# Two hand-overs of a fused attention and MoE kernel: weight pools freed in four parts, and a first output pair of eight plain products

## The chip, the cores and the metric

The kernel runs on one core of one Trainium2 chip. The metric is the device time of one execution in microseconds (us), less being better; all inputs start in the chip's memory and the output ends there. The core's engines are TensorE (PE in the profile), VectorE (DVE), ScalarE (ACT), GpSimd (POOL) and SyncE (SP), which mostly issues DMA transfers.

## The reference

Three stages, float32 in and out; the weights come as float64.

```python
B, H, S, D = 4, 8, 576, 64
scores = q @ k.T / sqrt(D) + min(bias(cumsum(max(s, 0))), 0)      # causal
x = softmax(scores) @ v            # to (2304 tokens, 512)
h = max(x @ w1, x @ w2, x @ w3)    # MoE1, three gates, d_ff 768
x = h @ w_out                      # (2304, 512)
a, b = x @ w_a, x @ w_b            # MoE2, d_ff 1536
out = (a * b) @ w_out2             # (2304, 512)
```

## The kernel before

**Products.** Each float32 operand is held as a rounded high part and the rest as a low part (`hi` and `lo`), and a product of two operands is three matmuls (hi·hi, hi·lo, lo·hi), added up in PSUM. The function `hilo` (L841) makes the two: `rnd` rounds on ACT (L81) or POOL (L88), then DVE subtracts (it is recorded at L839, as all of DVE's sums are).

**Stages.** Attention and MoE1 are interleaved until about 512 us. MoE1 keeps 22 of its 24 weight slabs (18 gate slabs, 6 of `w_out`; hi and lo of a slab are 4 KB in a partition) in one pool, `w1p` (L102, L247). For each block of 256 or 320 tokens it runs 18 gates of 12 matmuls (L555) and four `o` units of 18 (L582). Each `o` unit ends with an ACT copy into `xo` (L587) and a store by SP into the DRAM tensor `x2T` (L588). `xo` has two buffers, shared with the gates' `hf`.

MoE2's gates and the output are Strassen-Winograd products: of two 2x2 block matrices seven products are formed instead of eight, from sums of blocks that `a_side` and `b_side` make on DVE. MoE2 has 12 column blocks `c` and three token blocks `sb` of 768; a unit (c, sb) is a `Unit` (from L958) with the products 1, 2, 5, 6, 7, 4 and 3 of six matmuls with 384 columns. The products of one unit gather in three PSUM banks X, Y and Z with two buffers each: 1, 6, 7 and 4 go to X, 2 to Y, 5 and 3 to Z; between them ACT copies X out (`s1`, `u2`, `u3`; L981 to L987), and DVE adds. `emit` puts product 4 and 3 of the unit before between those of the next. A unit's two results are stored into `hT`, in DRAM (L1016, L1020).

x of token block 0 is split (`x2_part`) while MoE1 still runs. Those of blocks 1 and 2 (the halves of the tile `xt12`) are loaded at L909 in the first two units of MoE2, each with seven roundings, on ACT and POOL in turn, seven low parts and four sums on DVE. Their pools lie over `w1p`, and `xt12` also. w2(c), the weights of column block c, come as pairs of 32-bit words: a load into `wraw` (L825), an ACT pass (L828), two DVE passes (L831, L833), and `b_side` with POOL's roundings.

The output runs over nine pairs of 128-token blocks. `load_h` reads four pieces of `hT` into `hraw0` or `hraw1` (L1120), `prep_h` splits it with `a_side` into `slot` tiles, and seven products of 18 matmuls with 256 columns follow. Its weights (`wo32`, four blocks b11 to b22) are split by `b_side` into `woh1` to `wol7`.

**Order.** The kernel is written in program order with pools of tiles; a scheduler reorders the instructions by a simulated timeline, helped by `high_priority` blocks, and each engine then executes its list in order. A pool made with `reuse_waits="tile"` lets a new tile wait only for what lay under it; what was in one pool over several old ones waits per tile.

Of the kernel before, what the change touches and what calls it, by code (L numbers as in the profile page):

```python
# [29 lines left out]
def kernel(  # L30
# [29 lines left out]
    P = 128  # L60
# [41 lines left out]
    w1p = tc.alloc_tile_pool(name="w1p", bufs=1, side="left")  # L102
# [144 lines left out]
    w1_tiles(w1p, w1_keys[: NPRE - MF])  # L247
# [292 lines left out]
    def moe1_units(R, b, X):  # L540
# [31 lines left out]
        def outp(c):  # L572
# [15 lines left out]
            nc.sync.dma_start(x2T[c * P : (c + 1) * P, col : col + n], xo[:, :n])  # L588
# [212 lines left out]

    TB = 384
# [11 lines left out]
    def to_f32(src, outs):  # L814
# [23 lines left out]
    def tt(e, o, a, b, op):  # L838
        {"V": nc.vector, "P": nc.gpsimd}[e].tensor_tensor(o, a, b, op=op)  # L839

    def hilo(eng, hi, lo, src):  # L841
        rnd(eng, hi, src)
        tt("V", lo, src, f(hi), ALU.subtract)


# [82 lines left out]
    w1p.release()  # L928
# [361 lines left out]
```

## Time and profile before

| | us |
|---|---|
| median of 3 executions | 946.49 |
| lowest, highest | 943.96, 951.84 |
| the profiled execution | 949.84 |
| its span | 947.6 |
| PE busy | 904.0 (95% of the span) |
| DVE busy | 600.6 (63%) |
| ACT busy | 383.5 (40%) |
| POOL busy | 227.7 (24%) |

The profile is of one execution, and its times are on the clock of its span. A row of a chain of waits or a timeline names the engine, the line of the kernel, the operation and the tiles (out<-in), and says what the engine waited for before it. L839 and L81, L88 are helpers' lines, so the tile's name tells what the instruction is for. The granted clock is the share of TensorE's full speed that the chip granted in a stretch.

### The profile page before, as it was taken

Reading aid. Unit: us, or ns where it says so; the run is one execution under the profiler, and the core shown is the slowest. Engines: PE = TensorE matmul, PEld = TensorE weight load, DVE = VectorE, ACT = ScalarE, POOL = GpSimd, SP = SyncE. Lnnn points to the kernel's source line nnn. Section 1 sums busy time; section 2 is a strip of 40 time slices with the busy share of each in tenths; the row PEclk is TensorE's granted clock in tenths of the full one; section 3 lists DMA queues with packets and bytes.
Section 4 is the critical chain, followed back from the end, with each engine's and each line's share of the span. In section 5 each row is a group of like instructions: output and inputs, shape, how many; then the busy total and the mean of one; then the engine's idle time right before and its main releaser. Section 6 shows DMA issues by size and latency. Waiting matters only on the chain.

```text
span 947.6 us, 16918 instructions
## 1 busy us (share of the span) xinstructions
PE 904.0 (95%) x6182; PEld 841.6 (89%) x6182; DVE 600.6 (63%) x1416; ACT 383.5 (40%) x878; POOL 227.7 (24%) x331
## 2 busy tenths in 40 slices
PE   5899999999999999999999799999999998699998
PEld 4587789989999899999898699999999998699998
DVE  4787445554464644555563977666665779778874
ACT  4555644555455554555322323232322133233321
POOL 5454311222132221222111411111111212121220
PEclk9899999999999999999999999999999999799999
DMA  6655232313213132220314325353522131543431
GB/s 172 209 178 177 86 80 81 95 40 116 76 56 93 58 99 77 61 76 30 122 56 141 134 79 193 118 164 121 170 95 95 67 109 41 185 145 118 150 112 45
DMA packets 55210, 102.34 MB, mean 108 GB/s; under 512 B 5736, under 2 KB 39432, under 8 KB 55128
## 3 DMA queue, kind: packets, MB, share of 16 engines
q1 hardware_dynamic: 55128, 101.26, 34.0%
q8 instruction: 49, 0.80, 0.3%
q14 instruction: 33, 0.27, 0.1%
HBM read 77.29 MB, written 23.94 MB: 107 GB/s over the span
## 4 chain that ended last, share of the span: by engine, by line
PE 72%; DMA 12%; DVE 11%; issue 2%; ACT 1%; SPq 1%; POOL 0%; ACTq 0%; DVEq 0%
PE g L555 22%; PE X L952 15%; PE Z L952 7%; PE o L582 7%; PE fpv L500 5%; PE Y L952 4%; DMA wraw<-in_moe_w_b_dram 3%; DMA wraw<-in_moe_w_out_dram 3%; PE t L514 3%; PE f L435 2%; DVE u L839 2%; PE s L391 2%; DVE xl L839 2%; PE s L392 1%; DVE wl L839 1%
## 5 line engine op out<-in xcount | busy, mean ns | idle before, releaser
L555 PE MATMUL g<-Xh,hg 128*128 128x256 f32 (+1 forms) x576 | 176.3, 309 | 2.5 <-ACT hf L561 1.4
L555 PE MATMUL g<-Xl,hg 128*128 128x256 f32 (+1 forms) x576 | 174.9, 304 | 0.3 <-DVE Xl L92 0.2
L555 PE MATMUL g<-Xh,lg 128*128 128x256 f32 (+1 forms) x576 | 174.0, 303 | 0.0
L555 PEld LDWEIGHTS g<-Xh,hg 128*128 128x128 f32 x576 | 109.6, 191 | 6.6 <-ACT hf L561 1.6
L555 PEld LDWEIGHTS g<-Xl,hg 128*128 128x128 f32 x576 | 110.0, 191 | 3.0 <-DVE Xl L92 1.2
L555 PEld LDWEIGHTS g<-Xh,lg 128*128 128x128 f32 x576 | 109.8, 191 | 2.5 <-issue 2.3
L952 PE MATMUL X<-xh,wh 128*128 128x384 f32 x288 | 98.5, 342 | 8.3 <-ACT u L987 3.5
L952 PE MATMUL X<-xh,wl 128*128 128x384 f32 x288 | 97.3, 338 | 0.4 <-DVE wl L839 0.3
L952 PE MATMUL X<-xl,wh 128*128 128x384 f32 x288 | 97.0, 337 | 0.4 <-DVE xl L839 0.4
L88 POOL TENSOR_SCALAR wh<-wval 128x256 fp32r<-128x256 f32 x84 | 41.1, 499 | 218.2 <-PE Z L952 151.0
L952 PE MATMUL X<-woh,slot 128*128 128x256 f32 x432 | 83.5, 285 | 6.7 <-ACT slot L81 6.3
L564 DVE TENSOR_TENSOR hf<-g,hf 128x256 f32<-128x256 f32 (+1 forms) x96 | 43.7, 455 | 60.3 <-PE g L555 55.7
L952 PEld LDWEIGHTS X<-woh,slot 128*128 128x128 f32 x432 | 69.8, 193 | 7.3 <-ACT slot L81 6.6
L839 DVE TENSOR_TENSOR slot<-hraw,slot 128x768 fp32r<-128x768 f32 x63 | 62.7, 1014 | 18.3 <-POOL slot L88 16.6
L384 POOL TENSOR_SCALAR P<-P,rs 128x128 f32<-128x128 f32 (+2 forms) x80 | 51.0, 642 | 92.1 <-DVE rs L380 63.1
L952 PEld LDWEIGHTS X<-xh,wh 128*128 128x128 f32 x288 | 54.1, 188 | 12.9 <-ACT u L987 4.7
L952 PE MATMUL X<-wol,slot 128*128 128x256 f32 x216 | 61.3, 285 | 0.0
L375 ACT ACTIVATE P<-P,nm 128x128 f32<-128x128 f32 (+2 forms) x80 | 46.5, 581 | 32.2 <-DVE nm L368 26.6
L88 POOL TENSOR_SCALAR slot<-hraw 128x768 fp32r<-128x768 f32 x27 | 27.6, 1022 | 129.0 <-DVE hraw L839 53.1
L582 PE MATMUL o<-hh,lo 128*128 128x256 f32 (+1 forms) x192 | 58.2, 309 | 0.0
L81 ACT ACTIVATE slot<-hraw 128x768 fp32r<-128x768 f32 x36 | 30.4, 847 | 68.1 <-DVE hraw L839 36.0
L582 PE MATMUL o<-hl,ho 128*128 128x256 f32 (+1 forms) x192 | 57.6, 303 | 0.0
(156 smaller groups left out, 2267.2 us busy)
## 6 DMA issues: line engine op xcount, KB each, us to landing
hT<-u SPq DMA_DIRECT2D x72, 192.0 KB
hraw<-hT SPq DMA_DIRECT2D x36, 384.0 KB
wraw<-in_moe_w_dram SPq DMA_DIRECT2D x18, 512.0 KB
wraw<-in_moe_w_out_dram SPq DMA_DIRECT2D x18, 512.0 KB
qvraw<-in_qv_dram SPq DMA_DIRECT2D x12, 640.0 KB
kraw<-in_kT_dram SPq DMA_DIRECT2D x24, 288.0 KB
wraw<-in_moe_w_a_dram SPq DMA_DIRECT2D x12, 512.0 KB
wraw<-in_moe_w_b_dram SPq DMA_DIRECT2D x12, 512.0 KB
```

The source lines that it names most:

```text
L81: nc.scalar.activation(o, i, AF.Copy, scale=scale)
L88: nc.gpsimd.tensor_scalar(o, i, scale, 1.0, op0=ALU.mult, op1=ALU.mult)
L375: nc.scalar.activation(pt[:, c0:c1], pt[:, c0:c1], AF.Exp, bias=first, scale=-1.0, accum_out=sm[:, g : g + 1],)
L384: nc.gpsimd.tensor_scalar(pt[:, c0:c1], pt[:, c0:c1], rs[:, g : g + 1], 1.0, op0=ALU.mult, op1=ALU.mult,)
L391: nc.tensor.matmul(ps, QA1[:, qs], KB1[:, h, ksl], start=True, stop=False)
L500: nc.tensor.matmul(ps[h * D : h * D + D, c0:n], w, x, start=(t == 0), stop=(t == len(mm[h]) - 1),)
L514: nc.tensor.transpose(ps[:, j * P : j * P + P], pt[:, j * P : j * P + P], ident)
L555: nc.tensor.matmul(ps[:, :n], w[:, kk, :], x[:, kk, :], start=(i == 0), stop=(i == len(mm) - 1),)
L564: nc.vector.tensor_tensor(hf, ps[:, :n], hf, op=ALU.max)
L582: nc.tensor.matmul(ps[:, :n], w[:, c, :], x[:, m, :n], start=(i == 0), stop=(i == len(mm) - 1),)
L839: {"V": nc.vector, "P": nc.gpsimd}[e].tensor_tensor(o, a, b, op=op)
L952: nc.tensor.matmul(ps[:, :n], w, x, start=(first and i == 0), stop=(i == len(mm) - 1), skip_group_check=not first,)
```

## The change

The diff is cut to what decides places and order. Its parts:

1. `w1p` becomes four pools of 6, 5, 7 and 4 slabs (24, 20, 28 and 16 KB), and the pools of MoE2 are placed over them so that `xt12` lies over the first, the second raw buffer, w2(1) and five of the seven products of x1 over the second and third; products 7 and 3 of x1 have a pool of their own over the fourth.
2. The stores into `x2T` are issued by ACT instead of SP.
3. A weight's raw load is a step of its own (`load_raw`); that of w2(2) is written ahead of MoE2. Weight tiles are one for each product.
4. x1 is rounded by POOL alone, x2 by ACT alone; x2's loads are written in the third unit, behind w2(2)'s load and x1's last split. Units (0,2) and (1,1) change places.
5. The output's first pair is eight plain products of split blocks, in four chains of 36 matmuls (`out_std`), with no sums of blocks; the Winograd pairs begin with the second. The tiles of the output have other places, `hraw1` among them, which lay over x2 and now lies over MoE2's first raw buffer and weights.

```diff
-    w1p = tc.alloc_tile_pool(name="w1p", bufs=1, side="left")
+    w1p = [tc.alloc_tile_pool(name=f"w1p{i}", bufs=1, side="left") for i in range(4)]
-    w1_tiles(w1p, w1_keys[: NPRE - MF])
+    for p_, n0, n1 in zip(w1p, (0, 6, 11, 18), (6, 11, 18, NPRE - MF)):
+        w1_tiles(p_, w1_keys[n0:n1])
...
             nc.scalar.copy(xo[:, :n], ps[:, :n])
-            nc.sync.dma_start(x2T[c * P : (c + 1) * P, col : col + n], xo[:, :n])
+            nc.scalar.dma_start(x2T[c * P : (c + 1) * P, col : col + n], xo[:, :n])
...
-    def to_f32(src, outs):
+    def load_raw(src):
         pool = rawp[nraw[0] % len(rawp)]
         nraw[0] += 1
         raw = pool.tile([P, WC, 2], I32, tag="raw", bufs=1, name="wraw")
+        rv = raw.rearrange("p c t -> p (c t)")
...
+        return raw, nc.sync.dma_start(rv, src.bitcast(I32))
+
+    def to_f32(raw, outs):
...
-        nc.sync.dma_start(raw.rearrange("p c t -> p (c t)"), src.bitcast(I32))
...
     def hilo(eng, hi, lo, src):
         rnd(eng, hi, src)
-        tt("V", lo, src, f(hi), ALU.subtract)
+        return tt("V", lo, src, f(hi), ALU.subtract)
+    def a_side(q, sp, part=(0, 1)):
...
+        if 0 in part:
+            sp(1, a11)
...
+        if 1 in part:
+            sp(6, a11)
...
+    w2raw = {}
+
+    def load_w2_raw(c):
+        w2raw[c] = [load_raw(src[c]) for src in (wa, wb)]
+        return w2raw[c][1][1].ins
...
-        hi, lo = (
-            pool.tile([P, 7, 2 * P], F32R, tag=f"w{x}", bufs=1, name=f"w{x}{c % 2}")
-            for x in "hl"
-        )
+        hi, lo = {}, {}
+        for i in OPS:
+            for d, x in ((hi, "h"), (lo, "l")):
+                d[i] = pool.tile(
+                    [P, 2 * P], F32R, tag=f"w{x}{i}", bufs=1, name=f"w{x}{i}_{c % 2}"
+                )
         v_ = rA.tile([P, 4, 2 * P], F32, tag="val", bufs=1, name="wval")
-        for src, s in ((wa, 0), (wb, 2)):
-            to_f32(src[c], [(v_[:, s : s + 2].rearrange("p s c -> p (s c)"), slice(0, WC))])
+        for n, src in enumerate((wa, wb)):
+            raw = w2raw[c][n] if c in w2raw else load_raw(src[c])
+            o = v_[:, 2 * n : 2 * n + 2].rearrange("p s c -> p (s c)")
+            to_f32(raw[0], [(o, slice(0, WC))])
...
         if sb not in xs:
-            xs[sb] = [
-                {i: xr[sb].tile([P, KH, TB], F32R, name=f"x{c}{sb}{i}") for i in OPS}
-                for c in "hl"
-            ]
+            xs[sb] = {}, {}
+            for i in (1, 2, 4, 6, 5, 7, 3):
+                pool = xr1b if sb == 1 and i in (7, 3) else xr[sb]
+                for d, c in zip(xs[sb], "hl"):
+                    d[i] = pool.tile([P, KH, TB], F32R, name=f"x{c}{sb}{i}")
...
-    w1p.release()
+    for p_ in reversed(w1p):
+        p_.release()
...
     wop = lpool("wop")
     xt12 = wop.tile([P, 2, 4, KH, TB], F32, tag="wo", name="xt12")
+    rawB = lpool("rawB")
+    rawB.tile([P, WC, 2], I32, tag="raw", bufs=1, name="raw1")
+    wpool[1] = lpool("wB")
     xr[1] = lpool("xr1")
+    xr1b = lpool("xr1b")
     tmpA = lpool("tmpA")
-    tmpA.tile([P, WC, 2], I32, tag="raw", bufs=1, name="raw1")
-    rawp.append(tmpA)
-    wpool[1] = lpool("wB")
     xr[2] = lpool("xr2")
     ps_w = lpool("ps_w", space=PSUM)
...
-    order = [(0, 0), (1, 0), (0, 1), (0, 2), (1, 1), (1, 2)]
+    done1 = []
+
+    def load_x1():
+        done1.append(x2_part(1, 0, KH, xt12[:, 0], "P"))
+
+    def load_x2():
+
+
+        with tc.issue_after(raw2), tc.issue_after(done1[0]):
+            x2_part(2, 0, KH, xt12[:, 1], "A")
+
+    order = [(0, 0), (1, 0), (0, 1), (1, 1), (0, 2), (1, 2)]
     load_w2(1)
+    rawp.append(rawB)
+    raw2 = load_w2_raw(2)
         extra = []
-        if n < 2:
-            extra.append(lambda n=n: x2_part(n + 1, 0, KH, xt12[:, n], "AP"))
+        if n == 0:
+            extra.append(load_x1)
+        if n == 2:
+            extra.append(load_x2)
...
+    slots = {}
+
+    def put(pool, i0, i1):
+        for i in range(i0, i1):
+            slots[i] = pool.tile([P, KO, P], F32R, name=f"slot{i}")
...
     rB1 = rpool("rB1")
-    wo_tiles(rB1, ("l6", "h6", "l5", "h5"))
-    rB1.tile([P, 1024], F32, name="pad1")
+    wo_tiles(rB1, ("h6", "l6"))
+    obs = ob_tiles(rB1, 0, 2)
+    hraw1 = rB1.tile([P, MF2, 2 * P], F32, name="hraw1")
     rB2 = rpool("rB2")
-    hraw = [rB2.tile([P, MF2, 2 * P], F32, name="hraw0")]
-    wo_tiles(rB2, ("h1", "l1", "h2", "l2", "h3"))
+    hraw = [rB2.tile([P, MF2, 2 * P], F32, name="hraw0"), hraw1]
+    wo_tiles(rB2, ("h1", "l1", "h2", "l2"))
+    lB0 = lpool("lB0")
+    wo_tiles(lB0, ("h5", "l5", "h4"))
     lB1 = lpool("lB1")
-    wo_tiles(lB1, ("l3",))
-    slots = [lB1.tile([P, KO, P], F32R, name=f"slot{i}") for i in range(12)]
+    put(lB1, 0, 8)
+    wo_tiles(lB1, ("h3", "l3"))
+
+    wo7_tiles(0)
     lB2 = lpool("lB2")
-    slots += [lB2.tile([P, KO, P], F32R, name=f"slot{i}") for i in range(12, 18)]
-    wo_tiles(lB2, ("h7", "l7", "h4", "l4"))
-    hraw.append(lB2.tile([P, MF2, 2 * P], F32, name="hraw1"))
+    put(lB2, 8, 18)
+    wo_tiles(lB2, ("l4",))
...
+    def prep_std(blocks, engs):
+
+        r = hraw[0]
+        for b, e in zip(blocks, engs):
+            c, k = b // 2 * P, b % 2 * KO
+            hilo(e, slots[2 * b], slots[2 * b + 1], r[:, k : k + KO, c : c + P])
+
+    def out_std():
+
+        gate = prev[0]
+        o = obs[0], obs[1]
+        t0 = porder[0] * 2 * P
+        banks = dict(zip(((0, 0), (0, 1), (1, 1), (1, 0)), "XYZX"))
+        for (r, c), b in banks.items():
+            ps = ps_w.tile([P, 512], F32, tag=b, bufs=2, name=b)
+            mm = []
+            for k2 in range(2):
+                i = {(0, 0): 1, (1, 0): 2, (0, 1): 0, (1, 1): 3}[k2, c]
+                hh, hl = slots[2 * (2 * r + k2)], slots[2 * (2 * r + k2) + 1]
+                wh, wl = wot[f"h{i}"], wot[f"l{i}"]
+                for k in range(KO):
+                    mm += [
+                        (hh[:, k], wh[:, k]), (hh[:, k], wl[:, k]), (hl[:, k], wh[:, k]),
+                    ]
+            chain(ps, True, 256, mm)
+            nc.scalar.copy(o[r][:, 256 * c : 256 * c + 256], ps[:, :256])
+            if (r, c) == (0, 0):
+                gate.prod(4)
+                gate.prod(3)
+            if (r, c) in ((0, 1), (1, 0)):
+                nc.sync.dma_start(out[t0 + r * P : t0 + r * P + P, :], o[r])
+        prev[:] = []
-    with tc.high_priority(180):
+    with tc.high_priority(190):
         load_h(0)
         sp_wo("A", 1, b11)
         sp_wo("P", 2, b21)
+    with tc.high_priority(140):
+        prep_std((0, 1), "AA")
+        sp_wo("P", 0, b12)
+        sp_wo("A", 3, b22)
+        load_h(1)
+    with tc.high_priority(100):
+        prep_std((3, 2), "PA")
         tt("V", b11, b12, b11, ALU.subtract)
         tt("V", b12, b22, b12, ALU.subtract)
-    with tc.high_priority(90):
-        sp_wo("A", 3, b22)
         tt("V", b22, b22, b11, ALU.subtract)
         tt("V", b21, b21, b22, ALU.subtract)
-    with tc.high_priority(70):
-        prep_h(0)
-    with tc.high_priority(40):
-        sp_wo("A", 6, b22)
-        sp_wo("P", 5, b11)
+    nslot[0] = 8
+    out_std()
+    with tc.high_priority(60):
+        prep_h(1, (0,))
+        sp_wo("P", 6, b22)
+        prep_h(1, (1,))
+        sp_wo("A", 5, b11)
+    wo7_tiles(7)
     with tc.high_priority(10):
-        sp_wo("A", 7, b12)
-        sp_wo("P", 4, b21)
-        load_h(1)
-    for j in range(NPR):
+        sp_wo("P", 7, b12)
+        sp_wo("A", 4, b21)
+    load_h(2)
+    for j in range(1, NPR):
         emit(outs(j))
         if j + 1 < NPR:
             prep_h(j + 1)
```

The queue of SP where MoE2 begins, before; `xt12` with 128x2x384 is x1, then x2, `wraw_6296` and `wraw_6672` are raw parts of w2:

```order
L588 DMA x2T_101<-xo_6192 128x320
L588 DMA x2T_101<-xo_6214 128x320
L825 DMA wraw_6296<-in_moe2_w_b_dram 128x1024
L588 DMA x2T_101<-xo_6236 128x320
L909 DMA xt12_6270<-x2T_101 128x2x384
L588 DMA x2T_101<-xo_6258 128x320
L909 DMA xt12_6270<-x2T_101 128x2x384 x7
L825 DMA wraw_6672<-in_moe2_w_b_dram 128x1024
```

The same place in the change (the x2T stores are now in ACT's list):

```order
L825 DMA wraw_6338<-in_moe2_w_b_dram 128x1024
L930 DMA xt12_6294<-x2T_110 128x2x384 x4
L825 DMA wraw_6361<-in_moe2_w_a_dram 128x1024
L825 DMA wraw_6363<-in_moe2_w_b_dram 128x1024
L930 DMA xt12_6294<-x2T_110 128x2x384 x2
L825 DMA wraw_6880<-in_moe2_w_a_dram 128x1024
L825 DMA wraw_6885<-in_moe2_w_b_dram 128x1024
L930 DMA xt12_6294<-x2T_110 128x2x384 x2
L1041 DMA hT_6317<-u3_6367 128x384
```

x1's four loads no longer stand behind x2T stores, x2's last two stand last, behind two raw loads of w2(3).

DVE where MoE2 begins, before; `s1`, `u3` are sums of units, `xl11` the low part of x1's product 1, `hl_5885` the last low part of MoE1:

```order
L92 TENSOR_TENSOR hl_5885<-hf_6141,hh_5884 128x320
L831 TENSOR_SCALAR wraw_6296<-wraw_6296 128x512
L839 TENSOR_TENSOR s1_6319<-Y_6330,s1_6319 128x384
L833 SCALAR_TENSOR_TENSOR wval_6290<-wraw_6296 128x512
L839 TENSOR_TENSOR xl11_6367<-xt12_6270,xh11_6360 128x768
L839 TENSOR_TENSOR wl1_6289<-wval_6290,wh1_6288 128x256 x3
L839 TENSOR_TENSOR wval_6290<-wval_6290 128x256
L839 TENSOR_TENSOR xl12_6368<-xt12_6270,xh12_6361 128x768
L839 TENSOR_TENSOR wval_6290<-wval_6290 128x256
L839 TENSOR_TENSOR u3_6321<-Z_6345,u3_6321 128x384
```

The change; `xl21` to `xl27` belong to x2:

```order
L847 TENSOR_TENSOR xl16_6413<-xt12_6294,xh16_6412 128x768
L847 TENSOR_TENSOR xl17_6417<-xt12_6294,xh17_6416 128x768
L847 TENSOR_TENSOR xl13_6419<-xt12_6294,xh13_6418 128x768
L847 TENSOR_TENSOR s1_6365<-Y_6376,s1_6365 128x384
L847 TENSOR_TENSOR xl21_6559<-xt12_6294,xh21_6558 128x768
L847 TENSOR_TENSOR xl22_6561<-xt12_6294,xh22_6560 128x768
L847 TENSOR_TENSOR xl24_6563<-xt12_6294,xh24_6562 128x768
L847 TENSOR_TENSOR s1_6442<-Y_6453,s1_6442 128x384
L847 TENSOR_TENSOR xt12_6294<-xt12_6294 128x768 x2
L847 TENSOR_TENSOR xl25_6567<-xt12_6294,xh25_6566 128x768
L847 TENSOR_TENSOR xt12_6294<-xt12_6294 128x768
L847 TENSOR_TENSOR xl27_6569<-xt12_6294,xh27_6568 128x768
```

x1's steps now end ahead of the first unit's `s1`; x2's stand between the sums of the first two units.

SP where the output begins, before; `hraw0` takes the first and third pair, `hraw1` the second:

```order
L1120 DMA hraw0_8862<-hT_6287 128x3x256 x3
L1020 DMA hT_6287<-u2_8556 128x384
L1120 DMA hraw0_8862<-hT_6287 128x3x256
L1016 DMA hT_6287<-u3_8615 128x384
L1020 DMA hT_6287<-u2_8614 128x384
L1016 DMA hT_6287<-u3_8673 128x384
L1020 DMA hT_6287<-u2_8672 128x384
L1016 DMA hT_6287<-u3_8731 128x384
L1120 DMA hraw1_8907<-hT_6287 128x3x256
L1020 DMA hT_6287<-u2_8730 128x384
L1120 DMA hraw1_8907<-hT_6287 128x3x256 x3
```

The change:

```order
L1182 DMA hraw0_9026<-hT_6317 128x3x256 x3
L1045 DMA hT_6317<-u2_8718 128x384
L1182 DMA hraw0_9026<-hT_6317 128x3x256
L1041 DMA hT_6317<-u3_8777 128x384
L1045 DMA hT_6317<-u2_8776 128x384
L1041 DMA hT_6317<-u3_8835 128x384
L1182 DMA hraw0_9026<-hT_6317 128x3x256 x2
L1045 DMA hT_6317<-u2_8834 128x384
L1182 DMA hraw0_9026<-hT_6317 128x3x256 x2
L1041 DMA hT_6317<-u3_8893 128x384
L1182 DMA hraw1_9022<-hT_6317 128x3x256 x4
```

`hraw0` is filled twice there, for the first and the third pair, and the second pair's four loads follow behind that and a store of `u3`.

## Rows read from the trace of the kernel before

**Rows 1.** The page's first line: span and instructions.
```profile
span 947.6 us, 16918 instructions
```

**Rows 2.** Busy us of each engine by stretch, instructions in brackets, granted clock.
```profile
core 0: us, PE busy (x) PEld busy (x) DVE busy (x) ACT busy (x) POOL busy (x), PEclk, DMA share, GB/s
...
100.00:455.00 355.00, 355.00 (x2669) 326.66 (x2668) 179.91 (x602) 191.57 (x492) 87.08 (x134) 1.00 0.25 73
...
513.00:552.00 39.00, 30.84 (x159) 26.94 (x159) 35.08 (x54) 14.38 (x24) 14.32 (x11) 1.00 0.46 157
552.00:780.00 228.00, 223.89 (x1267) 220.31 (x1266) 156.21 (x334) 62.94 (x121) 34.03 (x71) 1.00 0.38 124
780.00:820.00 40.00, 29.57 (x178) 28.43 (x177) 37.53 (x43) 12.90 (x19) 7.74 (x6) 0.83 0.36 119
```

**Rows 3.** Chain of waits, whole span: start, us, engine or transfer, line, count.
```profile
552.46 2.10 PE X L952 x12
...
797.25 1.67 DVE wol L839
...
805.27 7.16 DMA hraw<-hT
...
828.67 2.15 PE X L952 x18
```

**Rows 4.** Waits of PE, 513 to 552: us in all, times, longest; the largest.
```profile
PE Z L952 <- DVE u L839: 2.3, 2, 1.7
```

**Rows 5.** Chain of waits that ends at 600, from 450 on.
```profile
474.90 2.35 DMA xt<-x2T
...
487.04 14.20 PE g L555 x95
...
512.45 4.58 DMA xt<-x2T
...
520.86 0.87 DVE xl L839
...
540.22 0.47 DVE u L839
```

**Rows 6.** Waits of PE, 780 to 820.
```profile
PE X L952 <- ACT slot L81: 6.3, 1, 6.3
PE Y L952 <- ACT slot L81: 3.0, 1, 3.0
PE X L952 <- ACT u L987: 0.9, 1, 0.9
```

**Rows 7.** Waits of ACT, 780 to 835; the largest.
```profile
ACT slot L81 <- DMA hraw<-hT: 9.6, 2, 6.6
```

**Rows 8.** Timeline of SP, three places: start, us, issues of DMAs.
```profile
463.37 1.22 SPq L588 DMA_DIRECT2D x2T<-xo  x1
...
513.17 0.33 SPq L588 DMA_DIRECT2D x2T<-xo  x1
...
804.10 1.72 SPq L1120 DMA_DIRECT2D hraw<-hT  x3
```

**Rows 9.** Two stretches behind the output's start, columns as in rows 2.
```profile
814.00:818.70 4.70, 4.70 (x24) 4.70 (x24) 4.70 (x7) 1.22 (x2) 0.00 (x0) 0.50 0.47 166
820.00:824.70 4.70, 4.70 (x42) 4.70 (x41) 2.35 (x4) 0.37 (x1) 0.84 (x1) 1.00 0.00 0
```

**Rows 10.** Timeline of ACT, 512 to 522: start, us, instruction, idle before.
```profile
512.72 0.43 ACT L587 COPY xo<-o 128x320 f32<-128x320 f32 x1 [0.67 <-PE o L582]
...
517.05 0.84 ACT L81 ACTIVATE xh<-xt 128x768 fp32r<-128x768 f32 x1 [1.94 <-DMA xt<-x2T]
...
519.67 0.48 ACT L987 COPY u<-X 128x384 f32<-128x384 f32 x1 [1.41 <-PE X L952]
```

**Rows 11.** Timeline of POOL, 516 to 540: two roundings of x.
```profile
518.56 1.02 POOL L88 TENSOR_SCALAR xh<-xt 128x768 fp32r<-128x768 f32 x1 [2.06 <-DMA xt<-x2T]
...
532.17 4.02 POOL L88 TENSOR_SCALAR xh<-xt 128x768 fp32r<-128x768 f32 x1 [4.96 <-DVE xt L839]
```

More of the change, by code (lines that the diff above doesn't have):

```diff
@@ L818, in to_f32 @@
         raw = pool.tile([P, WC, 2], I32, tag="raw", bufs=1, name="wraw")
+        rv = raw.rearrange("p c t -> p (c t)")
+        if not wide:
+            return raw, nc.sync.dma_start(rv[:, :WC].bitcast(F32), src)
+        return raw, nc.sync.dma_start(rv, src.bitcast(I32))
+    def to_f32(raw, outs):
         if not wide:
             rv = raw.rearrange("p c t -> p (c t)")[:, :WC].bitcast(F32)
-            nc.sync.dma_start(rv, src)
             for o, c in outs:
@@ L910, in x2_part @@
         cnt = [0]
+        last = []
         def sp(i, src):
@@ L914, in sp @@
             cnt[0] += 1
-            hilo(e, hi[i][:, k0:k1], lo[i][:, k0:k1], src)
+            last.append(hilo(e, hi[i][:, k0:k1], lo[i][:, k0:k1], src).ins)
         a_side([q[:, n] for n in range(4)], sp)
+        return last[-1]
     def load_x0():
@@ L1001, in mms @@
         def mms(i):
-            wh, wl = w2[c][0][:, i - 1], w2[c][1][:, i - 1]
+            wh, wl = w2[c][0][i], w2[c][1][i]
             xh, xl = xs[sb][0][i], xs[sb][1][i]
@@ L1047, in load_wo @@
         s = 0 if k < KO else 2
[L1049 removed]
+        to_f32(load_raw(w2o[k])[0], [
             (wo32[0][:, s + d, k % KO], slice(256 * d, 256 * d + 256)) for d in range(2)
         ])
[L1053 removed]
+    done1 = []
[5 more added lines that the diff above has]
+    order = [(0, 0), (1, 0), (0, 1), (1, 1), (0, 2), (1, 2)]
     order += [(c, sb) for c in range(2, MF2 - 2) for sb in range(NSB)]
@@ L1073 @@
     xr[2].release()
+    tmpA.release()
+    xr1b.release()
+    xr[1].release()
     wpool[1].release()
-    tmpA.release()
-    xr[1].release()
+    rawB.release()
     xr[0].release()
@@ L1122, in load_h, with prep_h @@
             )
-    def prep_h(j):
+    def prep_h(j, part=(0, 1)):
         r = hraw[j % 2]
-        hi, lo = {}, {}
         eng = dict(zip((1, 2, 4, 6, 5, 7, 3), "AAPAAPP"))
-        for i in OPS:
-            for d in (hi, lo):
-                d[i] = slots[nslot[0] % NSLOT]
-                nslot[0] += 1
+        if j not in hts:
+            hts[j] = hi, lo = {}, {}
+            for i in OPS:
+                for d in (hi, lo):
+                    d[i] = slots[nslot[0] % NSLOT]
+                    nslot[0] += 1
+        hi, lo = hts[j]
         def sp(i, src):
             hilo(eng[i], hi[i], lo[i], src)
-        a_side((r[:, :KO, :P], r[:, KO:, :P], r[:, :KO, P:], r[:, KO:, P:]), sp)
-        hts[j] = hi, lo
+        a_side((r[:, :KO, :P], r[:, KO:, :P], r[:, :KO, P:], r[:, KO:, P:]), sp, part)
     def outs(j):
@@ L1198 @@
     lB1.release()
+    lB0.release()
     wop.release()
```

37 lines of the change are left out of this document (20 added, 17 removed).

## The prediction

> **What bounds the kernel now.** I read the head of the page first, then the table of busy time by stretch, since one share for the whole span mixes stages. The span is 947.6 us [rows 1] and the profiled execution took 949.84, 2.24 more. It stands 3.35 above the median, 946.49; the sum is made against 949.84 and 3.35 is taken off at the end. Runs of this kernel spread over 944 to 952, so about 1% (9.5 us) is what a measurement can tell from no change.
>
> In the table [rows 2] the reader is to see TensorE (PE) busy 355.00 of 355.00 us from 100 to 455: no other engine bounds there. From 552 to 780 it is busy 223.89 of 228. Two stretches stand out, 513 to 552 with 30.84 of 39 and 780 to 820 with 29.57 of 40. In both one stage hands over to the next, and what this change can gain lies in these two.
>
> *Start of MoE2.* In the chain of waits a matmul of 384 columns is 2.10/12 = 0.175 us when PE is fed [rows 3]. The 159 of 513 to 552 need 27.8 us, so **11.2 us** are lost. The view of PE's waits shows there no one cause but many small ones, the largest 2.3 in two pieces on a sum by DVE [rows 4]; DVE is busy 35.08 of 39, ACT and POOL well below half [rows 2]. DVE is the bound: x1, x2 and w2(1) are all split there. In the chain of that stretch x1's loads are issued at 512.45, after the last MoE1 unit has freed the one weight pool [rows 5], though their columns were stored long before.
>
> *Start of output.* PE is idle 40 - 29.57 = 10.4 us [rows 2], of which 6.3 and 3.0 are waits on roundings by ACT (`slot`) and 0.9 one on a copy [rows 6]. ACT itself waits 9.6 for `hraw` [rows 7]: the second pair's loads stand on SP behind hT stores, are issued from 804.10 on [rows 8], and land 7.16 after issue [rows 3]. Behind this idling the granted clock of 814.0 to 818.7 is 0.50 (1.2 GHz): 24 matmuls where 42 of the same kind fit in 4.7 us at 1.00 (2.4 GHz) [rows 9]. That is 4.7 x (1 - 24/42) = 2.0, with the edges 2.3. The loss is 10.4 + 2.3 = **12.7 us**.
>
> **The change, part by part.**
>
> *MoE2's start: 11.2 becomes 4.5, so -6.7.* PE goes through 95 gate matmuls in 14.20 us [rows 5], 12 x 0.149 = 1.79 a gate. The gates end at 501 to 503, so the sixth of 18, last user of the first of the four pools, ends near 503 - 12 x 1.79 = 481.5. x1's loads now need that alone, 31 us earlier. x1's 11 wide DVE instructions (7 splits, 4 sums) at 0.87 [rows 5] are 9.6 us, and most of them leave 513 to 552 for a stretch where DVE has room (179.91 of 355) [rows 2]. Only products 7 and 3 still need what the last o unit holds. w2(1)'s splits go ahead likewise. What stays is x2, whose last half cannot be read before the last x2T stores have landed. The last xo copy ends at 512.72 + 0.43 = 513.15 [rows 10], its store's issue takes 0.33 [rows 8]. No row has that store's landing alone; I take the x2T reads on either side, 2.35 and 4.58 [rows 5], the short one for the store and both for the load, with 0.4 for its issue. Store landed 515.9, load 518.6 to 520.8. Then in line: ACT's rounding (0.84), DVE's split (0.87), DVE's `s1` sum (0.47), six of DVE (four sums, two splits) at 0.87 to 526.0 to 528.2, ACT's last rounding and its copy (0.84 + 0.48) [rows 5, 10]. So the copy of the second unit's product 7 is done at 527.3 to 529.5, and PE wants it after 78 matmuls, at 512.5 + 13.65 = 526.2. That wait is 1.0 to 3.2; I take 2.0, the middle, and 2.5 for short ones, as before. What is queued matters here: ACT waits for x2's last load inside its own order, with the copies that free PE's banks behind it.
>
> *Output's start: 12.7 becomes 4.7, so -8.0.* Call T the first plain product. The four chains are 4 x 36 matmuls where a Winograd pair has 7 x 18: 18 more, at the 2.15 that 18 take [rows 3], **+2.15 us**. With 18 late gate matmuls between they run 20.2 us. The second pair's loads still stand on SP behind the third pair's and an hT store that DVE frees near T + 3.7. Issued at T + 4.1 and landed 7.16 later [rows 3], T + 11.3, they leave seven DVE steps of 0.47 or 0.87 to T + 16.5, where PE wants product 1 at T + 20.2. Product 5 stands behind three weight splits at 1.67 [rows 3]: ready at T + 24, wanted at T + 25.2. So the same 7.16 us are covered with 1 to 4 to spare. Left are 0.9 where product 7 follows product 6 in its bank at once (as now [rows 6]), 0.6 for the last plain operand, 1.0 for what slips, and the 2.15: 4.7. With the idling gone I expect no stretch at 0.50, so those 2.3 go too.
>
> *x2T stores on ACT: +0.5.* 32 issues leave SP, of which the longest took 1.22 [rows 8]: at most 32 x 1.22 = 39 us of ACT exposed; at least nothing, since ACT is busy 191.57 of 355 there and PE is never idle [rows 2]. Below nothing too, by a little: SP's weight loads no longer stand behind a store that waits for its copy. ACT issues right behind its own copy, so it waits for that copy's end alone; behind it stand the gates' copies. I take 0.5, near the low end, since PE has work in hand in that stretch.
>
> *Middle: +1.0.* The new order of units puts products 7 and 4 of one bank six matmuls (1.05 us) apart in 23 places, before mostly 12 or 18. Where they touch, the wait is 0.9 [rows 6], so six cover it, unless an ACT rounding of 0.84 [rows 10] stands in front of the copy. Bounds: -3 (most of the 4.1 idle of this stretch goes [rows 2]) and 23 x 0.42 = +10 (half a rounding each time). I take +1.0, near the row.
>
> Weight tiles by operand, raw loads issued ahead, the releases: nothing by themselves, hidden under DVE's and ACT's idle time before 513. One load (w2(3)) now stands on ACT and DVE ahead of MoE1's last `hh` rounding; if it is late PE waits at the last o unit for what is left of it, within the range.
>
> **A rule against it.** x1 is rounded by POOL alone now. Among idle neighbours a rounding took 1.02, among back-to-back DVE instructions 4.02 [rows 11]. By the first, x1's seven are done before 513 but for products 7 and 3, and the sum stands; by the second, see rival 1. The Trainium skill, SBUF — State Buffer, section "Who interferes with whom", says that a DVE instruction with two SBUF inputs and a GpSimd instruction that reads SBUF keep each other out for the whole instruction. The trace agrees with that (4.02 against 1.02).
>
> **Sum.** -6.7 - 8.0 + 0.5 + 1.0 = -13.2; 949.84 - 13.2 = 936.6, in terms of the median 936.6 - 3.35 = **933**. All low ends (2.0 left at MoE2's start, 2.0 at the output's, -3 in the middle): -9.2 - 10.7 - 3.0 = -22.9, so 923.6. All high ends of this case (+1.2, +4, +3): 941.
>
> **The rivals.**
> 1. *x1 and x2 serialize.* POOL and DVE go one after the other: 7 x 1.02 + 11 x 0.87 = 16.7 us for x1; the last ones fall behind 513 and push x2's steps, which hold ACT and DVE in order ahead of PE's copies. If x1 begins at 503 instead of 492, 16.7 - 10 = 6.7 come back: 933 + 6.7 = **940**. For: DVE also has MoE1's sums there. Against: loads by 490. Chance 0.14.
> 2. *The second pair's loads land late again*, so the output part does not do what it says: PE idles some 6, the clock falls again, 2.15 come on top. Of the 8.0 nothing is left: 933 + 8 = **941**. For: these loads stand last on SP. Against: 20 us of plain products. Chance 0.12.
> 3. *Copies at a distance of six* stall half a rounding each: 933 - 1 + 10 = **942**. Against: two units alternated before as well, with 4.1 us idle in 228. Chance 0.09.
> 4. *Slower: ACT's queue holds the gates.* Each store's issue stands ahead of copies that free MoE1's banks. The time passes 956 when each of 32 costs PE (956 - 933)/32 = 0.72 us; at the longest issue seen, 1.22, it is 933 + 39 = **972**. For: ACT executes in order. Against: PE was never idle from 100 to 455. Chance 0.05.
>
> The forecast has 0.60.
>
> **The numbers.** The likeliest is 933. The low end, 923, is all low ends together. The high end, 945, takes in rivals 1 to 3 with their own spread; beyond lie rival 4 and two rivals at once, some 0.12, and below 923 some 0.05. Faster by over 1% is under 937.0: most of the forecast (0.56 of 0.60) and the mild forms of rivals 1 and 2 (0.06): 0.62. Slower by over 1% is over 956: rival 4 and 0.02 for all else: 0.07. Within: 0.31.
>
> **What would show it.** In the profile after: x1's loads at 482 to 490 and its DVE work before 513; in the 39 us after the first MoE2 matmul DVE's share well under 0.9 and PE idle 4 to 5 us. At the output four runs of 36, `hraw1` landed some 9 us before the second pair's first matmul, no 0.50 clock, PE idle under 3. Store issues among ACT's rows and no PE wait on `hf` or `xo`. The prediction is wrong if PE waits for ACT copies in dozens of places, if the lower clock shows again at the output, or if the gates before 513 take longer than now.

## The result, and the profile after

| | before | after |
|---|---|---|
| median of 10 executions, us | 945.16 | 937.64 |
| lowest, highest | 943.55, 951.84 | 931.61, 939.93 |
| profiled execution, its span | 949.84, 947.6 | 932.05, 930.3 |

The ratio is 0.9899, 95% interval 0.9878 to 0.9919: about 1% faster, inside the range foretold and 4.6 us above the forecast of 933. The profiled execution of the change is one of its fastest, that of before one of its slowest; so the profiles differ by 17.8 us and the medians by 7.5. The head of the page of the change, with the row of the granted clock:

```profile
span 930.3 us, 17019 instructions
...
PE 898.9 (97%) x6200; PEld 840.8 (90%) x6200; DVE 597.4 (64%) x1407; ACT 382.7 (41%) x876; POOL 226.9 (24%) x331
...
PEclk9999999999999999999999999999999999999999
```

To see where the time went I cut both spans at the same work: at the first MoE2 matmul, the 301st and the 1401st (a count is off by one or two where a matmul straddles a cut). The columns are those of [rows 2]. First before, then the change:

```profile
0.00:512.47 512.47, 495.51 (x3536) 442.17 (x3537) 282.54 (x879) 257.86 (x653) 147.41 (x220) 0.99 0.32 95
512.47:576.40 63.93, 55.77 (x302) 51.87 (x301) 53.39 (x95) 20.73 (x36) 18.89 (x22) 1.00 0.44 152
576.40:775.53 199.13, 195.02 (x1101) 191.44 (x1101) 134.07 (x290) 55.65 (x107) 29.47 (x61) 1.00 0.37 122
775.53:947.60 172.07, 157.70 (x1247) 156.16 (x1246) 130.62 (x153) 49.26 (x83) 31.94 (x29) 0.96 0.35 113
```

```profile
0.00:509.95 509.95, 493.76 (x3536) 440.88 (x3537) 297.62 (x905) 261.32 (x657) 154.07 (x230) 1.00 0.35 104
509.95:564.60 54.65, 53.38 (x302) 52.41 (x301) 37.96 (x65) 15.69 (x29) 8.62 (x14) 1.00 0.23 75
564.60:765.98 201.38, 194.21 (x1101) 191.58 (x1101) 135.57 (x296) 57.33 (x109) 30.80 (x62) 1.00 0.38 128
765.98:930.30 164.32, 157.51 (x1265) 155.92 (x1264) 126.26 (x144) 48.39 (x82) 33.38 (x27) 1.00 0.37 118
```

The reader is to take the second number of each row, the stretch's length. **MoE2's first 300 matmuls** went from 63.93 to 54.65 us, -9.3 (foretold -6.7). **The 1100 behind them** went from 199.13 to 201.38, +2.2 (foretold +1.0). **The rest with the output** went from 172.07 to 164.32, -7.7 (foretold -8.0), though with 18 matmuls more. **Attention and MoE1** went from 512.47 to 509.95, -2.5, and this is not the change's: in the profile of before the clock fell early in attention. These are one row of each profile:

```profile
40.00:50.00 10.00, 9.96 (x36) 6.64 (x35) 9.48 (x28) 4.91 (x12) 4.29 (x6) 0.54 0.55 177
```

```profile
40.00:50.00 10.00, 9.31 (x56) 6.68 (x57) 9.82 (x29) 6.02 (x15) 4.41 (x6) 1.00 0.58 183
```

36 matmuls against 56 in the same 10 us; 10 x (1 - 36/56) = 3.6 us. So that stretch is some 1.1 us slower in the change, and the sum without the chance of the clock is +1.1 - 9.3 + 2.2 - 7.7 = -13.7, where -13.2 was foretold. That the median moved by less has its cause, as far as the profiles show it, in the clock of the middle, below.

PE's waits in MoE2's start and its middle, in the change; the last line is the largest of the middle before:

```profile
PE X L977 <- ACT u L1012: 0.8, 2, 0.4
PE X L977 <- ACT u L1010: 0.4, 1, 0.4
```

```profile
PE X L977 <- ACT u L1012: 6.9, 3, 3.2
```

```profile
PE X L952 <- ACT u L987: 2.0, 3, 0.9
```

At the start 1.2 us are left where [rows 4] is the largest of many. In the middle stand 6.9 in three pieces on the copy `u3` behind product 7, two of about 3 us (3.22 and 2.90); before, no wait there was longer than 0.9 us. What held ACT for the first of them, in the timelines of SP, ACT and PE:

```profile
610.15 2.11 SPq L825 DMA_DIRECT2D wraw<-in_moe_w_out_dram  x2
```

```profile
611.21 0.48 ACT L1010 COPY u<-X 128x384 f32<-128x384 f32 x1 [1.62 <-PE X L977]
614.16 0.69 ACT L836 ACTIVATE wraw<-wraw 128x512 f32<-128x512 f32 x1 [2.47 <-DMA wraw<-in_moe_w_out_dram]
616.43 0.69 ACT L836 ACTIVATE wraw<-wraw 128x512 f32<-128x512 f32 x1 [1.58 <-DMA wraw<-in_moe_w_out_dram]
617.02 0.85 ACT L1012 COPY u<-X 128x384 f32<-128x384 f32 x2
```

```profile
617.54 0.45 PE L977 MATMUL X<-xh,wh 128*128 128x384 f32 x1 [3.22 <-ACT u L1012]
```

SP issues two loads of `w_out`'s raw words at 610.15, when the raw buffers come free. ACT executes in order, and its passes over those words (L836) stand ahead of the two copies. ACT waits 2.47 and 1.58 for the loads, the copies start at 617.02, and PE has nothing else: two units run in step, so both X banks wait for their product 7 to be copied at once. The output's start, PE's waits and the second pair's loads [rows 6, 8]:

```profile
PE Z L977 <- ACT slot L81: 1.2, 1, 1.2
PE X L977 <- ACT u L1010: 1.1, 2, 0.6
```

```profile
786.68 2.08 SPq L1182 DMA_DIRECT2D hraw<-hT  x4
```

The loads of `hraw1` go out 1.9 us behind the first plain product (784.8), where T + 4.1 was reckoned, and one wait of 1.2 on `slot` is left of 9.3.

### The profile page after: what moved, and what is told of

It is laid out like the page before. It is cut to its first block, busy times and chain, and to the rows that moved or that the text cites. A ratio compares the mean times of both kernels' runs of the same rounds, so it can differ in the third digit from the quotient of the medians.

```text
span 930.3 us, 17019 instructions
## 1 busy us (share of the span) xinstructions
PE 898.9 (97%) x6200; PEld 840.8 (90%) x6200; DVE 597.4 (64%) x1407; ACT 382.7 (41%) x876; POOL 226.9 (24%) x331
## 4 chain that ended last, share of the span: by engine, by line
PE 83%; DMA 9%; DVE 4%; issue 1%; ACT 1%; SPq 1%; POOL 0%; ACTq 0%; DVEq 0%
PE g L557 23%; PE X L977 20%; PE Z L977 11%; PE o L584 7%; PE fpv L502 5%; PE Y L977 5%; PE t L516 3%; DMA wraw<-in_moe_w_out_dram 2%; DMA wraw<-in_moe_w_b_dram 2%; PE f L437 2%; PE s L393 2%; PE s L394 1%; DMA xt<-x2T 1%; DMA wraw<-in_moe_w_dram 1%; PE ft L479 1%
## 5 line engine op out<-in xcount | busy, mean ns | idle before, releaser
L977 PE MATMUL X<-woh,slot 128*128 128x256 f32 x432 | 81.2, 281 | 0.5 <-ACT ob L1012 0.5
L977 PEld LDWEIGHTS X<-xh,wh 128*128 128x128 f32 x288 | 54.1, 188 | 13.7 <-ACT u L1012 9.3
L584 PE MATMUL o<-hh,ho 128*128 128x256 f32 (+1 forms) x192 | 57.0, 304 | 0.3 <-ACT xo L589 0.3
L370 DVE CUSTOM_DVE_ANT_0 P<-s,maskJ 128x128 f32<-128x128 f32 (+2 forms) x80 | 40.5, 514 | 25.2 <-PE s L394 19.2
```

The lines of the kernel that those rows point to most:

```text
L370: nc.vector.tensor_tensor_reduce(pt[:, c0 : c0 + w], v_, m_, -scale, first, op0=ALU.add, op1=ALU.min, accum_out=nm[:, i : i + 1],)
L584: nc.tensor.matmul(ps[:, :n], w[:, c, :], x[:, m, :n], start=(i == 0), stop=(i == len(mm) - 1),)
L977: nc.tensor.matmul(ps[:, :n], w, x, start=(first and i == 0), stop=(i == len(mm) - 1), skip_group_check=not first,)
```

## The experiments

All are the change with the edit shown. Times are medians; intervals are those of the ratio to the kernel before, run on the same chip.

**The change again.** 

> The changed kernel once more, unaltered, for a second profile and for the clock of every execution. Theory 1 (the two hand-overs gained 17 us less 3 of a clock drop between 40 and 50 us that only the profile of before had; the rest of the spread is the clock): executions with a mean clock of 1.00 take 930 to 933, those with 0.99 take 936 to 940, and the second profile, if it is one of these, shows its half-clock stretch in one place of 4 to 10 us. Rival (the spread is in the waits, in the middle or at the hand-overs, and the clock follows them): two profiles differ by several us of PE's waits on ACT, with the clock the same.

Measured: 936.48, 0.9895 (0.9876 to 0.9915). The second profile differs from the first in one place, behind the second of the two waits; the third and fourth row are its middle and its rest:

```profile
664.00:668.00 4.00, 3.18 (x10) 3.18 (x11) 2.61 (x7) 1.82 (x4) 0.00 (x0) 0.50 0.69 222
668.00:672.00 4.00, 4.00 (x18) 4.00 (x17) 2.01 (x6) 0.70 (x1) 0.00 (x0) 0.68 0.35 132
...
563.72:768.29 204.57, 197.02 (x1101) 194.16 (x1101) 135.58 (x296) 57.16 (x109) 30.80 (x62) 0.98 0.37 126
768.29:931.90 163.61, 157.48 (x1265) 155.89 (x1264) 126.36 (x144) 48.35 (x82) 32.71 (x27) 1.00 0.37 119
```

PE waits 3.2 us, and then the clock granted is 0.50 (1.2 GHz) for 4 us and partly for 4 more; the middle takes 204.57, 3.2 more than in the first profile. So both theories have a part: the waits are nearly the same in both profiles (6.9 and 6.5 us on the copies), and the clock falls behind one of them in one profile. In the 16 executions of the change those at a mean clock of 0.998 to 1.00 took 931.6 to 932.7, those at 0.990 to 0.996 took 933.7 to 939.9.

**Stores on SP again.**
```diff
-            nc.scalar.dma_start(x2T[c * P : (c + 1) * P, col : col + n], xo[:, :n])
+            nc.sync.dma_start(x2T[c * P : (c + 1) * P, col : col + n], xo[:, :n])
```


> x2T's 32 stores back on SP, all else as in the change. My step (ACT issue costs some 0.5 us in MoE1; SP keeps x2's last loads moving): within 3 us of the change, PE's waits on hf and xo in 100 to 512 fall from 3.3 us to about 2. Rival (the stores on SP hold weight loads and x1's loads, as the 30.3 us wait of SP before): x1's loads come late, MoE2's start loses 3 to 9 us again, time 3 to 9 us above the change.

Measured: 940.23, 0.9928 (0.9903 to 0.9952). The profile's stretches:

```profile
514.22:568.99 54.77, 53.10 (x302) 52.46 (x301) 38.49 (x66) 15.77 (x29) 8.71 (x14) 1.00 0.23 76
568.99:775.70 206.71, 198.84 (x1101) 195.84 (x1101) 135.68 (x296) 57.06 (x109) 31.08 (x62) 0.98 0.37 124
```

The first 300 matmuls take 54.77, as in the change: x1's loads came early with the stores on SP too, since in this list they stand ahead of the last stores (479.89 and 511.46), and the rival falls. Of my own step, too, a part fell: PE's waits on `hf` and `xo` are 3.5 us, against 3.3 in the change. The median is 3.7 above the change's of the same chip, but the profile puts its difference into the middle, whose clock is 0.98, and into the lower clock early in attention, neither of which the edit touches; with four timed executions I don't call the queue faster or slower by itself.

**A third raw buffer.**
```diff
+        if pool is None:
+            q = rA.tile([P, 4, 1, TB], F32, tag="xt", bufs=1, name="wraw")
+            q = q.rearrange("p a b t -> p (a b t)")[:, : 2 * WC].bitcast(I32)
+            raw = q.rearrange("p (c t) -> p c t", t=2)
...
-    rawp.append(rawB)
+    rawp += [rawB, None]
```


> A third buffer for raw weights (in the place of x0's staging tile, free by then), all else as in the change. Theory (the two waits of 3.2 us near 617 and 664 are ACT's weight pass, which stands ahead of the copies of product 7 and waits for a w_out load that could be issued only when a raw buffer came free): loads go out a unit earlier, both waits vanish, 552 to 780 loses 2 instead of 7.7 us, time 4 to 6 us under the change. Rival (six matmuls are too few for ACT's copy whatever stands ahead, or the queue is at fault and not the buffer): waits stay, time within 1.5 us of the change.

Measured: 930.76, 0.983 (0.981 to 0.985), 5.7 us under the change on the same chip, and outside its interval. Its middle, and what PE waits for there:

```profile
566.98:765.01 198.03, 194.30 (x1101) 191.40 (x1101) 133.28 (x292) 55.64 (x107) 30.65 (x62) 1.00 0.37 125
```

```profile
PE X L982 <- ACT u L1017: 2.9, 2, 1.7
PE Z L982 <- DVE u L852: 0.7, 2, 0.4
```

The waits on product 7's copy fall from 6.9 to 2.9, the middle from 201.38 to 198.03 with the clock at 1.00. So the buffer is the cause, but the theory holds in part only: the waits are halved and don't vanish. `w_out`'s loads go out singly (600.84, 613.88) where the change issued two at 610.15; one late pass stands ahead of the copies instead of two, and ACT still waits 3.23 us for its load. The median gains more than the 3.4 us of this middle. Its profile shows no low clock behind the waits that are left, which would explain the rest; the last run below shows that this is not always so.

**The first pair as a Winograd product.** The output's order as before, in the places of the change, but with the second pair's loads ahead of where they were.
```diff
-    out_std()
...
+    with tc.high_priority(140):
+        load_h(1)
...
+        prep_h(0)
...
-    for j in range(1, NPR):
+    for j in range(NPR):
```


> The first output pair by seven products with sums again, in the places and pools of the change, the second pair's loads at a higher priority than before. Theory (the eight products hide the loads and the splits of the second pair): PE's idle time at the output's start returns, 6 to 12 us, less 2.15 us of matmuls; time 5 to 11 us above the change, and the half clock shows behind it. Rival (the places alone, with hraw1 no longer over x2, made the gain): within 2 us of the change or 2 us below.

Measured: 941.18, 0.995 (0.9932 to 0.9967). Its rest with the output, and PE's waits:

```profile
770.08:939.10 169.02, 158.50 (x1247) 156.77 (x1246) 132.42 (x152) 50.29 (x84) 35.26 (x29) 0.98 0.35 115
```

```profile
PE X L977 <- ACT slot L81: 3.1, 1, 3.1
PE Y L977 <- ACT slot L81: 1.8, 1, 1.8
```

169.02 us against 164.32 in the change and 172.07 before, with 3.1 and 1.8 of the waits on `slot` back [rows 6] and a clock of 0.98. So of the 7.7 us the places and the earlier loads bring 3.1, the eight products 4.7 net of their 18 matmuls, by one profile each and with the lower clock behind the waits counted in. Theory and rival each have a part.

**One pool for MoE1's slabs.**
```diff
-    w1p = [tc.alloc_tile_pool(name=f"w1p{i}", bufs=1, side="left") for i in range(4)]
+    w1p = [tc.alloc_tile_pool(name="w1p", bufs=1, side="left")]
```


> MoE1's 22 weight slabs in one pool again, released at once, all else as in the change. My step (x1's early loads are what took 9.3 us out of the start of MoE2): x1's loads go out at 510 or later, the first 300 matmuls of MoE2 take 60 to 64 us where the change takes 54.7, time 5 to 9 us above the change. Rival (the single engines for x1's and x2's roundings and the loads of w2(2) ahead did it): under 2 us above the change.

Measured: 934.23, 0.9881 (0.9852 to 0.9911). The first 300 matmuls, and SP:

```profile
510.03:565.35 55.32, 53.41 (x302) 52.35 (x301) 45.29 (x75) 17.42 (x32) 11.11 (x16) 1.00 0.34 115
```

```profile
483.22 3.20 SPq L929 DMA_DIRECT2D xt<-x2T  x3
```

The first low part of x1 on DVE, in this run and in the change:

```profile
512.38 2.45 DVE L846 TENSOR_TENSOR xl<-xt,xh 128x768 fp32r<-128x768 f32 x2
```

```profile
502.12 0.95 DVE L847 TENSOR_TENSOR xl<-xt,xh 128x768 fp32r<-128x768 f32 x1
```

My step falls here, in two ways. With one pool three of x1's loads go out at 483 all the same (in the change all four, from 478.10): a new tile waits for the tiles under it, not for the pool. And x1's DVE steps don't come early: SP issues no further load until 509.08, the steps begin at 512.38, behind MoE2's first matmul, and yet the stretch takes 55.32, only 0.7 more. DVE is busy 45.29 of 55.32 us there, nearly as full as before (53.39 of 63.93). What has left the stretch, against before, are the splits of w2(1), which DVE runs from 502.03 on.

**The old order of units.**
```diff
-    order = [(0, 0), (1, 0), (0, 1), (1, 1), (0, 2), (1, 2)]
+    order = [(0, 0), (1, 0), (0, 1), (0, 2), (1, 1), (1, 2)]
```


> Units (0,2) and (1,1) in their old order, all else as in the change. Theory (the new order of units pairs two units so that ACT's weight pass falls between products 7 and 4, and so makes the two waits of 3 us in the middle): waits on the copy of product 7 in 552 to 780 fall from 6.9 us to 2, time 3 to 6 us under the change, less what x2 then costs at MoE2's start (0 to 3). Rival (raw loads with two buffers are late in either order): the waits stay, time within 2 us of the change or above it.

Measured: 936.15, 0.9894 (0.9866 to 0.9921). Waits in the middle:

```profile
PE X L977 <- ACT u L1012: 7.7, 4, 2.6
```

They stay, so the order of these two units doesn't make them; the first 300 matmuls take 56.21.

**Both engines for the roundings.**
```diff
-        done1.append(x2_part(1, 0, KH, xt12[:, 0], "P"))
+        done1.append(x2_part(1, 0, KH, xt12[:, 0], "AP"))
...
-            x2_part(2, 0, KH, xt12[:, 1], "A")
+            x2_part(2, 0, KH, xt12[:, 1], "AP")
```


> x1's and x2's roundings on ACT and POOL in turn, as before, all else as in the change. By the rows of POOL (three roundings in 3.27 us, three more in 3.92 beside DVE) x1 on POOL alone takes near 1.1 to 1.5 each and ends ahead of x2's need: no difference, within 1.5 us of the change. Rival (POOL and DVE shut each other out and x1's splits end at 515 for that): x1's last split ends 2 to 4 us earlier and the time falls by 1 to 2 us; or x2, with POOL's roundings beside DVE's sums at 4 us each, comes late and costs 2 to 5 us.

Measured: 936.85, 0.9906 (0.9873 to 0.9939): no difference in the median, in five executions from 934.6 to 943.1. In its profile, which is of the slowest, the first 300 take 57.62, 3.0 more. PE waits there once, 3.25 us, for a copy that stands in ACT's list behind a rounding of x2; two of DVE's sums ahead of that took 1.58 and 1.57 us beside POOL's roundings, against 0.95 in the change. Some 1.7 of the 3.0 (57.62 x 0.03) is the clock, 0.97. So the second half of the rival shows in this profile.

**Loads one slab earlier, with the third buffer.**
```diff
...
-            extra.append(lambda k=wo_next: load_wo(k))
+            extra.append(lambda k=wo_next: (load_wo(k), pre_wo(k + 1)))
```


> Third raw buffer, and each w_out slab's raw load written one slab ahead of its conversion. Theory (what is left of the two waits, 1.84 and 1.36 us with the third buffer, is still the landing of a w_out load): both vanish, the middle loses under 1.5 us, time 2 to 4 us under the one with the third buffer alone, 926 to 929. Rival (the scheduler puts the conversions where they stall the copies whatever the loads do): within 1 us of it, or other waits of 1 to 2 us.

Measured: 933.16, 0.9875 (0.9841 to 0.9908). The theory falls; the waits in its middle moved, and the middle takes 205.20 us at a clock of 0.98:

```profile
PE X L982 <- ACT u L1017: 3.3, 2, 1.9
PE X L982 <- ACT s L1011: 2.4, 1, 2.4
```

**One pool and stores on SP together.**
```diff
+    w1p = [tc.alloc_tile_pool(name="w1p", bufs=1, side="left")]
...
+            nc.sync.dma_start(x2T[c * P : (c + 1) * P, col : col + n], xo[:, :n])
```


> One pool for MoE1's slabs and x2T's stores on SP, both at once, all else as in the change; each alone cost nothing in the first 300 MoE2 matmuls (54.8 us and 54.8 us against 54.7). Theory (either alone lets x1's loads out by 484, since the loads are only held by stores ahead of them on SP, and by the list's order; with both undone they go out behind the last stores at 512): x1's loads at 511 to 518, its splits from 517 on, the first 300 matmuls take 58 to 63 us, time 3 to 8 us above the change. Rival (x1's early loads are not what counts at all; w2(1)'s early splits and x2 behind x1 are): loads late, but the first 300 matmuls still under 57 us.

Measured: 939.91, 0.9939 (0.9916 to 0.9961). The first 300 matmuls, and SP:

```profile
509.87:569.95 60.08, 55.16 (x302) 53.94 (x301) 47.97 (x81) 17.60 (x32) 13.48 (x19) 0.97 0.38 132
```

```profile
509.82 0.43 SPq L929 DMA_DIRECT2D xt<-x2T  x1
510.57 0.33 SPq L589 DMA_DIRECT2D x2T<-xo  x1
510.95 4.43 SPq L929 DMA_DIRECT2D xt<-x2T  x7
```

With both undone x1's loads stand behind the stores again, and the stretch takes 60.08, 5.4 more than in the change (some 1.8 of it the clock of 0.97) and 4.8 more than with one pool alone. Either of the two parts lets the loads out; both absent, they wait. A raw load of w2 waits with them (508.01, against 482.82 with one pool alone), and DVE waits 6.97 us for it, with the last splits of w2(1) behind it in its list; what of the 5.4 is x1's and what is w2's is not separated.

**MoE2's start undone.** Besides, x2 in the second unit, both engines, the old order of units, no raw load ahead.
```diff
...
-        if n == 2:
+        if n == 1:
             extra.append(load_x2)
...
+    rawp.append(rawB)
     load_w2(1)
-    rawp.append(rawB)
-    raw2 = load_w2_raw(2)
```


> As the run with one pool and stores on SP, and besides x2 loaded in the second unit again, both engines for x1 and x2, the units in their old order, and w2(2)'s raw load not ahead: MoE2's start as before but for the places of the tiles and one weight tile for each product. Theory: the first 300 matmuls take 62 to 65 us, as before (63.9), time 7 to 11 us above the change. Rival (the places alone, with w2(1) and its raw buffer over slabs that are free early, make most of the gain): under 59 us.

Measured: 940.42, 0.9944 (0.9923 to 0.9965). Start and middle:

```profile
508.46:572.72 64.26, 56.59 (x302) 52.82 (x301) 53.26 (x95) 21.77 (x38) 16.56 (x23) 0.97 0.45 151
572.72:771.04 198.32, 194.21 (x1100) 191.74 (x1101) 131.00 (x286) 53.79 (x104) 30.88 (x60) 1.00 0.36 119
```

64.26 us, as before (63.93), with some 1.9 of it the clock of 0.97: the places of the tiles alone bring 1.6 at most. Loads that don't stand behind the stores bring 5.4 of the 9.3, with the clock counted in, and the later x2 with what goes along (most splits of w2(1) stand behind 510 here) the other 4. Its middle takes 198.32, without a wait of over 1.1 us: here the two units don't run in step, and one unit's products stand between the other's 7 and 4.

**Third buffer, old order of units.**
```diff
...
-    order = [(0, 0), (1, 0), (0, 1), (1, 1), (0, 2), (1, 2)]
+    order = [(0, 0), (1, 0), (0, 1), (0, 2), (1, 1), (1, 2)]
...
-    rawp.append(rawB)
+    rawp += [rawB, None]
```


> Third raw buffer with units (0,2) and (1,1) in their old order. Theory (the third buffer takes the two waits of 3 us away in either order, the old order costs 1 us at MoE2's start): 929 to 933, the same as the third buffer alone within 2 us, no wait over 2 us in the middle. Rival (in the old order the waits on product 7's copy are of another kind, seven of up to 2.6 us, and stay): 934 to 937.

Measured: 929.26, 0.9833 (0.9804 to 0.9862), the same as the third buffer alone within the intervals. The two are the fastest of this study, 1.7% under the kernel before. As foretold, no wait of over 2 us stands in the middle. But its profile, the slowest of its six executions (935.08), shows the lower clock there all the same: the middle, and a stretch behind waits of 1.64 and 0.72 us:

```profile
564.12:769.66 205.54, 199.38 (x1101) 197.43 (x1101) 129.47 (x277) 53.29 (x103) 28.61 (x58) 0.97 0.33 113
```

```profile
668.00:672.00 4.00, 4.00 (x12) 4.00 (x13) 2.58 (x5) 0.89 (x2) 0.00 (x0) 0.50 0.39 153
```

So the third buffer shortens the waits, and the clock can fall behind the shorter ones too. Four of these six executions had a mean clock of 0.998 or more and took 928.0 to 929.4; of the change it was four of sixteen.

## Why the prediction was right, and where not

**Where the time lies.** Right: all of the gain is in the two hand-overs, 17.0 us in the profiles by the rows above.

**MoE2's start, -6.7.** Right in place, low by 2.6: the wait of 2.0 for x2 was 0.4. Its chain ran as reckoned: x2T's last store landed 2.97 us after its issue and x2's last load 3.03, and the copy of the second unit's product 7 was done 15.6 us after the first MoE2 matmul, where 14.8 to 17.0 was reckoned. PE asked for it at 15.3 and not at 13.65, since its 78 matmuls and two short waits ahead took longer. In all PE waited 1.2 us there.

**The reason given for it failed, in two steps.** "x1's loads now need that alone": they needed no more with one pool either, and what had held them was SP's list, with the stores ahead. A store waited 30.3 us there for its copy, the loads behind it:

```profile
SPq L588 <- ACT xo L587: 32.0, 4, 30.3
```

I read the 512.45 of [rows 5] as the pool's release because it came right behind the last unit. The run with both parts undone shows the stores to be the cause, and the one with the stores back on SP that the four pools act through the list: its loads stand ahead of the stores. The second step is that most of x1's DVE instructions "leave 513 to 552". In the change they do, but with one pool they stay, and the stretch takes only 0.7 more. DVE was the bound, as read: its busy time in the stretch goes with the stretch's length, 53.4 us with 63.9 before, 48.0 with 60.1 (one pool and stores on SP), 45.3 with 55.3 (one pool) and 38.0 with 54.7 (the change). But the first 8 us off DVE brought all but 0.7, and with one pool these were the splits of w2(1), for which the prediction has one sentence and no price; x1's came on top for little. No run leaves the splits of w2(1) alone behind, so their part is argued from these rows and not shown by itself.

**Output's start, -8.0.** Right, -7.7; the loads' landing was covered, as reckoned, with 1.2 us of waits on `slot` left of 9.3, and so the second rival falls. In all eleven profiles with the eight products this stretch took 163.6 to 165.8 us at a clock of 1.00. The Winograd run puts 4.7 of the gain down to the eight products.

**Stores on ACT, +0.5.** The first stretch is 1.1 slower in the one profile, which is within its spread: at a clock of 1.00 it took 508.6 to 510.8 in six profiles with the stores on ACT, and 508.5 and 509.9 in the two with them on SP (MoE2's start undone, and one pool with them). So the term is too small to be seen, and the fourth rival falls. PE's waits on `hf` and `xo`, which were to be none, are there, but with the stores on SP they are no smaller:

```profile
PE g L557 <- ACT hf L563: 1.9, 2, 1.3
PE g L557 <- ACT xo L589: 1.1, 1, 1.1
```

**Middle, +1.0.** This is the step that failed in size: +2.2 in the profile that kept its clock, +5.4 in the second, and with it the median lies 4.6 above the forecast. The third rival had the place (copies with six matmuls between) and not the cause: not a rounding of 0.84 in front, 23 times, but twice a pass that waits for a DMA, which the term did not ask about. Nor did it reckon what the clock takes behind such a wait. Of the eight profiles with two raw buffers and these waits, six show a clock of 0.97 or 0.98 in the middle and 204.6 to 208.8 us; the two at 1.00 take 201.4 and 201.8.

That the sum came near is luck in part: MoE2's start brought 2.6 more than reckoned, and the middle took 1.2 to 4.4 more.

**The rule on POOL and DVE.** x1's roundings took 1.1 to 1.5 us each, none near the 4.02 of [rows 11]. The 1.02 of those rows did not stand among idle neighbours, as I had it: a low part of w2 on DVE ran beside it and took 1.04 where the next ones took 0.41. x1's splits did end only at 515, behind w2(3)'s raw pass in DVE's list, and PE did not wait for them. The Trainium skill's rule (SBUF — State Buffer, "Who interferes with whom") cost nothing in the change that the total shows. The run with both engines agrees with it, in sums of 1.57 us beside POOL's roundings where the change shows 0.95.

What stays open: why most of these schedules put two units in step, and the kernel before and the run with MoE2's start undone do not, how the 5.4 us of the loads divide between x1 and w2, and how the other 4 divide between x2's place, the engines, the raw load of w2(2) and the splits of w2(1).

## What to carry to other kernels

Ask of every wait, not only those of 3 us, what the clock did behind it: taking 4.0 us off the waits of the middle brought 5.7 in the median. On an engine that executes in order, a pass over data still on its way holds all copies behind it, so the load that feeds such a pass wants a buffer that is free early; a third buffer did that, and writing the load earlier in the program added nothing. Before a late load is put down to a pool or a buffer, look at the row ahead of it on its queue. And an experiment that leaves the supposed cause undone, as the one pool left x1's DVE work where it was, can show that the gain had another.

## What the runs showed of the hardware

Behind PE's waits of 2.5 to 3.2 us the granted clock fell to 0.50 in one profile of the same program and stayed at 1.00 in the other; with the third buffer it fell behind 1.64 and 0.72 us in one profile and not behind 1.67 in another. The same holds for a stretch at 40 to 52 us in attention, where it fell in six of thirteen profiles. Executions of the one program lay between 931.6 and 939.9, the fast ones at the higher mean clock; only stretches with the same work and the same clock compare.
